# A cosine attention and gated MLP kernel on one core: the second half of each output tile is copied by ScalarE, and the planner may pick TensorE work out of order

## The chip, the cores and the metric

The kernel runs on one core of one Trainium2 chip. The metric is the device time in microseconds (us) of one launch. A profile of one execution gives what each engine did: TensorE (PE, its weight loads PEld), VectorE (DVE), ScalarE (ACT), GpSimd (POOL) and SyncE (SP), which issues most of the DMAs.

## The reference

The first part is attention with normalised queries and keys; the second is a two-matrix MLP with a gate of its own.

```python
q_n = q / (norm(q) + 1e-6);  k_n = k / (norm(k) + 1e-6)    # q, k, v: (8, 12, 448, 64)
attn = softmax(q_n @ k_n.T / tau)                          # tau = 0.1
x = (attn @ v).transpose(0, 2, 1, 3).reshape(3584, 768)
h = x @ w_in                                               # w_in: (768, 2048)
out = (h * cos(h)) @ w_out                                 # w_out: (2048, 768), out: (3584, 768) float32
```

## The kernel before, in words

**Work units.** There are 8 batches of 448 rows. The 12 heads of a batch are taken two at a time, which makes 48 pairs, six to a batch, numbered g = 0 to 47. For each pair, `scores` issues one short and three long groups of matmuls into the two PSUM buffers SC0 and SC1, and ScalarE exponentiates each group into the tile PX (L707). One pair later `attend` multiplies PX by the values into the PSUM buffer AV: two short groups R (L730) and three groups AV (L737), and the sums of the softmax beside them (L745, L753 and others). VectorE or ScalarE copies AV out to the tile xu; the reciprocals of the sums go through DRAM and come back spread over the partitions as the tile RB; GpSimd multiplies the two into the tile xT, the transposed input of the MLP (L877).

**The MLP.** When a batch's six xT pieces are done, and some pairs later, `m1` multiplies them by the first matrix (called M1 here; L887, full 128x128 matmuls), ScalarE takes the cosine (L916) and VectorE multiplies it in, giving the tile gT. The second matrix product (M2) works on 28 output tiles of 128 rows by 768 columns. M2 is the filler: `m2_fill` puts some steps of it between the score and attention groups of each pair. In the pairs the M2 steps are written for 64x64 quarters of TensorE (`m2_quarters`, L985): one step is four rows of 64x64 matmuls on both halves of the tile. The two halves (384 columns each) lie in the two banks of the one PSUM buffer MP, called PO and TP, and there is no second buffer for them. Near the end M2 uses full-size matmuls and more banks (L1014).

**The drain.** When the last step of tile t is done, `m2_drain` copies half 0 and half 1 from PSUM to the tile osb, and the DMA to the output (L956, issued by SyncE) waits for both halves. Both copies are VectorE instructions (L952), except the last piece of the last tile (t = 27), which ScalarE takes (L950). The first step of the next tile needs PO and TP, so it waits for both copies.

**The order.** Every instruction group is an `Op` with an engine, a cost in us, the tiles that it reads and writes, and for TensorE a mode: "Q" for 64x64 quarters, "C32" for 128x32 columns (AV and the sums), "F" for full size. `play` plans the whole program by these costs, engine by engine; `emit` writes the streams in the planned order with semaphore waits where tiles demand them. The order on ScalarE, VectorE, GpSimd and SyncE comes from due times (`o.late`), which are worked back from the planned TensorE starts in three passes. TensorE takes its operations in the order in which the program lists them: in the first stage (`free`, about the first 57 us: the first batch, its M1 and the loads) the planner may choose among the next 24, later it takes the head of the list alone. A choice is made by planned start: an operation further on is taken only if it starts more than `PATIENCE` = 0.1 us before the ones ahead of it. A change of mode costs `SWITCH` = 0.124, 0.094 or 0.107 us (into Q, C32, F) in the plan. `settled` adds a wait of `SETTLE` = 0.2 us after an earlier operation; it stands between the two R groups of a pair, and between the first and second half of a tile's M2 steps in quarters.

Of the kernel before, what the change touches and what calls it, by code (L numbers as in the profile page):

```python
# [6 lines left out]
ACT = mybir.ActivationFunctionType  # L7
# [5 lines left out]

PLAN = {
    "apart": 1,
    "ahead": (1, 2),
    "folded": (0, 1, 2, 3),
    "grid": {2: (16, 5, 6), 3: (11, 3, 4), 4: (8, 2, 3)},
# [44 lines left out]
class Program:  # L63
# [7 lines left out]
    DRAIN = {"ACT": 0.21, "DVE": 0.28, "POOL": 0.25, "SP": 0.3, "PE": 0.0}  # L71
    OVERLAP = {"ACT": 0.09, "DVE": 0.08, "POOL": 0.0, "SP": 0.0, "PE": 0.0}
    WINDOW = 24
    PATIENCE = 0.1
    TAKEOFF = {"SP": 1.85, "ACT": 1.85, "POOL": 1.6}
    LANDING = 0.45
# [79 lines left out]
    def play(self):  # L156
        ops = self.ops
        left = [len(o.deps) for o in ops]
        ready_at = [0.0] * len(ops)
        users = [[] for _ in ops]  # L160
        for o in ops:
            for y, k in o.deps:
                users[y.idx].append((o, k))
        free = {e: 0.0 for e in self.ENGINES}
        free["PE"] = free["SP"] = 0.7
        mode, port = None, 0.0
        flows = {"hw": [], "sw": []}
        clock = warm = 0.0
        self.gaps = []
        pe = [o for o in ops if o.eng == "PE"]  # L170
        waiting = {e: [] for e in self.ENGINES}
        for o in ops:
            if left[o.idx] == 0:
                waiting[o.eng].append(o)
        todo = len(ops)
        flying = held = 0
        room_at = 0.0

        def release(o, issued=False):
            for w, k in users[o.idx]:  # L180
                if o.dma is not None and (k is None) != issued:
                    continue
                left[w.idx] -= 1
                r = o.start if k is None else o.end + (self.SETTLE if k == "settled" else self.latency(o, w))
                if r > ready_at[w.idx]:
                    ready_at[w.idx] = r
                if left[w.idx] == 0:
                    waiting[w.eng].append(w)

        def flow(until):  # L190
            nonlocal clock, flying, held, room_at
            while clock < until:
                heads = [q[0] for q in flows.values() if q and q[0][0] <= clock + 1e-9]
                step = until - clock
                for q in flows.values():
                    if q and q[0][0] > clock + 1e-9:
                        step = min(step, q[0][0] - clock)
                total = sum(h[2] for h in heads) / (self.BOTH if len(heads) > 1 else 1.0)
                for h in heads:
                    step = min(step, h[1] * total / h[2])  # L200
                clock += step
                done = []
                for h in heads:
                    h[1] -= step * h[2] / total
                for q in flows.values():
                    if q and q[0][1] <= 1e-9:
                        done.append(q.pop(0))
                for h in done:
                    flying -= 1
                    if h[3].eng == "SP":  # L210
                        held -= h[3].descs // h[3].nd
                        room_at = clock + self.LANDING
                    if h[4]:
                        h[3].end = clock + self.LANDING
                        release(h[3])
                if done:
                    return True
            return False

        while todo:  # L220
            best = None
            for e in self.ENGINES:
                if e == "PE":
                    s = None
                    for o in pe[: self.WINDOW if pe and pe[0].free else 1]:
                        if o.free != pe[0].free:
                            break
                        if left[o.idx] == 0:
                            t = max(free[e], ready_at[o.idx])
                            if s is None or t < s - self.PATIENCE:  # L230
                                s, c = t, (t, 0, o)
                    if s is None:
                        continue
                else:
                    if not waiting[e]:
                        continue
                    f = free[e]
                    now = min(max(f, ready_at[o.idx]) for o in waiting[e])
                    o = min((o for o in waiting[e] if ready_at[o.idx] <= now + 1e-9), key=lambda o: (o.late, o.idx))
                    s = now  # L240
                    for w in waiting[e]:
                        if w.late < o.late - PLAN["margin"] and ready_at[w.idx] <= now + min(PLAN["hold"], 0.5 * o.cost):
                            o, s = w, max(f, ready_at[w.idx])
                    if e == "SP" and held and held + o.descs > self.ROOM:
                        continue
                    if e == "SP" and held + 2 * o.descs > self.ROOM:
                        s = max(s, room_at)
                    if o.lock:
                        s = max(s, port)
                    c = (s, 1, o)  # L250
                if best is None or c[:2] < best[:2]:
                    best = c
            if flying and flow(best[0] if best is not None else 1e9):
                continue
            s, _, o = best
            e = o.eng
            if e == "PE":
                pe.remove(o)
                if o.free:
                    self.gaps.append((max(free[e], 3.0), s))  # L260
                if mode is not None and mode != o.mode:
                    s += self.SWITCH[o.mode]
                mode = o.mode
            else:
                waiting[e].remove(o)
            o.start = s
            o.end = s + o.cost
            free[e] = max(free[e], o.end - self.OVERLAP[e])
            if o.lock:
                port = o.end  # L270
            todo -= 1
            if o.dma is None:
                release(o)
                continue
            release(o, True)
            clock = max(clock, s) if not flying else clock
            s += self.TAKEOFF[e] + o.lead
            if e == "POOL" and warm == 0.0:
                warm = s + self.COLD
            for n in range(o.nd):  # L280
                flows["sw" if e == "POOL" else "hw"].append(
                    [max(s + n * o.cost / o.nd, warm if e == "POOL" else 0.0), max(o.bulk / o.nd, 0.02), o.weight, o, n + 1 == o.nd])
                flying += 1
                if e == "SP":
                    held += o.descs // o.nd
        while flying:
            flow(1e9)
        self.span = max(o.end for o in ops)
# [102 lines left out]
def bass_cosine_attention__then__act_gcu_kernel(  # L391
# [10 lines left out]
    DM = NH * D  # L402
# [32 lines left out]
    def sbs(name, n, shape, dt):  # L435
        return [sb("%s%d" % (name, i), shape, dt) for i in range(n)]
# [22 lines left out]
    osb = sbs("osb", 3, [128, DM], F32)  # L459
# [486 lines left out]
    def m2_drain(t, hf, name, po, w):  # L946
        o, n, ends = t % 3, w[1] - w[0], t == B * S // 128 - 1
        dst, keys = osb[o].ap()[:, w[0] : w[1]], [("osb", o, y) for y in range(2)]
        if ends and w[1] == DM:
            act(lambda e: e.activation(dst, po[:, 0:n], ACT.Copy, bias=0.0), name + [("osb", o, 0)], [("osb", o, hf)], n, label="osb%d" % t)  # L950
        else:
            dve(lambda e: e.tensor_copy(dst, po[:, 0:n]), name, [("osb", o, hf)], n, label="osb%d" % t)  # L952
        if not ends and hf == 0:
            return
        c0, c1 = w if ends else (0, DM)
        fns = [lambda e, p0=p0, row=row: e.dma_start(  # L956
            bass.AP(out.tensor, row * DM + c0, [[NB * DM, BP], [1, c1 - c0]]), osb[o].ap()[p0 : p0 + BP, c0:c1]) for p0, row in segments(t)]
        for x, eng in enumerate(("SP", "ACT") if ends and hf else ("SP",)):
            dma(eng, fns[x : x + 1] if ends and hf else fns, [("osb", o, hf)] if ends else keys, [], "last" if x else "out%d" % o,
                n / DM if ends else 1.0, "out%d" % t, None, 1.0)  # L960
# [294 lines left out]
```

## Time and profile before

| | |
|---|---|
| median of 3 runs | 425.53 us (424.62 to 425.71) |
| span of the profiled execution | 424.5 us (the only time that the records give for it) |
| TensorE busy | 414.0 us, 98% |
| ScalarE busy | 274.1 us, 65% |
| VectorE busy | 189.0 us, 45% |
| GpSimd busy | 236.9 us, 56% |
| granted TensorE clock | 1.000 |
| copies to osb | VectorE 56, ScalarE 1 |

The span runs from the first to the last instruction. A group row of the profile gives an instruction's source line, engine, operation, output and input tiles with their shapes, the count, then the busy time, the mean duration in ns, and the idle time of the engine before it with what ended it. TensorE's busy share counts overlapping matmuls as busy, so small stalls between groups are seen better in the starts of successive groups than in the share.

### The profile page before, as it was taken

The numbers are of one execution on the slowest core, as the hardware profiler recorded it, in microseconds if no ns is written. First come the engines' busy times: TensorE is split into PE (matmuls) and PEld (weight loads), VectorE is DVE, ScalarE is ACT, GpSimd is POOL, SyncE is SP. The second block draws the span as 40 slices with busy tenths as digits, with TensorE's granted clock in tenths as the row PEclk, the third lists the DMA queues.
The fourth block names the chain that finished last, engine by engine and source line by source line (L and its number), as shares of the span: only waits on it lengthen the run. The fifth ranks groups of instructions, "written<-read, shape, count | busy, mean of one in ns | idle before, by whom it ended". The sixth has DMA issues, their size and how long they took to land.

```text
span 424.5 us, 13591 instructions
## 1 busy us (share of the span) xinstructions
PE 414.0 (98%) x6077; PEld 234.8 (55%) x6077; DVE 189.0 (45%) x250; ACT 274.1 (65%) x363; POOL 236.9 (56%) x189
## 2 busy tenths in 40 slices
PE   8899989999999999999999999999999999999997
PEld 3454556655556555655566455655566545555565
DVE  4564744555653086225733078122852144223521
ACT  5896578884897557876588556775488735713500
POOL 4999996897833794927493395806856042020000
PEclk9999999999999999999999999999999999999999
DMA  8999999999576999589655996569955930141023
GB/s 188 250 253 224 207 215 161 195 206 231 102 107 144 201 223 186 116 193 209 155 116 86 207 229 106 133 100 224 224 111 89 147 105 2 42 120 38 2 60 90
DMA packets 81034, 63.61 MB, mean 150 GB/s; under 512 B 45776, under 2 KB 75984, under 8 KB 80976
## 3 DMA queue, kind: packets, MB, share of 16 engines
q1 hardware_dynamic: 62768, 50.06, 56.8%
q0 software_dynamic: 18048, 12.59, 19.7%
q8 instruction: 48, 0.79, 0.8%
q10 hardware_dynamic: 160, 0.10, 0.1%
q14 instruction: 10, 0.08, 0.1%
HBM read 54.98 MB, written 11.13 MB: 156 GB/s over the span
## 4 chain that ended last, share of the span: by engine, by line
PE 73%; POOL 8%; DMA 6%; issue 4%; ACT 4%; SPq 3%; DVE 2%; ACTq 0%; POOLq 0%; DVEq 0%
PE MP L985 18%; PE SC L887 17%; PE AV L887 11%; PE SC L692 5%; PE AV L737 5%; POOL qks L643 4%; PE MP L1014 4%; POOL xT L877 3%; PE SC L1014 3%; DMA RB<-scr 3%; PE MP L887 2%; PE AV L730 2%; PE AV L763 1%; DMA qkT<-qks 1%; ACT PX L707 1%
## 5 line engine op out<-in xcount | busy, mean ns | idle before, releaser
L707 ACT ACTIVATE PX<-SC 128x448 bf16<-128x448 f32 (+1 forms) x192 | 153.2, 823 | 25.8 <-PE SC L692 15.6
L985 PE MATMUL MP<-W,gT 64*64 64x384 bf16 x2816 | 142.0, 323 | 0.8 <-DVE qkT L681 0.6
L985 PEld LDWEIGHTS MP<-W,gT 64*64 64x64 bf16 x2816 | 78.7, 107 | 34.5 <-issue 3.5
L643 POOL TENSOR_TENSOR qks<-raw,rn 128x896 bf16<-128x896 f32 (+1 forms) x48 | 79.6, 1680 | 31.8 <-ACT rn L635 31.6
L887 PE MATMUL SC<-xT,W 128*128 128x448 bf16 x444 | 90.2, 352 | 0.0
L877 POOL TENSOR_TENSOR xT<-xu,RB 128x448 bf16<-128x448 f32 x34 | 37.7, 1136 | 74.7 <-DMA RB<-scr 74.7
L604 POOL TENSOR_TENSOR sq<-raw 128x896 bf16<-128x896 f32 x44 | 73.8, 1694 | 8.3 <-DMA raw<-in_q_dram 7.7
L916 ACT ACTIVATE cosb<-SC,cst 128x896 f32<-128x896 f32 x37 | 37.2, 1006 | 49.0 <-PE SC L887 44.5
L887 PEld LDWEIGHTS SC<-xT,W 128*128 128x128 bf16 x444 | 43.4, 98 | 40.2
L887 PE MATMUL AV<-xT,W 128*128 128x448 bf16 x276 | 59.7, 353 | 1.7 <-POOL xT L877 1.7
L952 DVE COPY osb<-MP 128x384 f32<-128x384 f32 x50 | 25.9, 552 | 67.0 <-PE MP L985 56.4
L611 DVE TENSOR_REDUCE n<-sq 128x14 f32<-128x896 bf16 (+2 forms) x49 | 51.4, 1055 | 6.3 <-ACT sq L602 5.2
L692 PE MATMUL SC<-qkT 64*64 64x448 bf16 x576 | 52.1, 357 | 0.4 <-ACT PX L707 0.2
L918 DVE TENSOR_TENSOR gT<-SC,cosb 128x896 bf16<-128x896 f32 x37 | 40.3, 1088 | 23.2 <-ACT cosb L916 23.1
L916 ACT ACTIVATE cosb<-AV,cst 128x896 f32<-128x896 f32 x23 | 23.1, 1006 | 35.0 <-PE AV L887 32.0
L887 PEld LDWEIGHTS AV<-xT,W 128*128 128x128 bf16 x276 | 26.0, 98 | 29.1 <-POOL xT L877 5.1
L918 DVE TENSOR_TENSOR gT<-AV,cosb 128x896 bf16<-128x896 f32 x23 | 25.0, 1088 | 27.5 <-ACT cosb L916 27.4
L817 DVE COPY xu<-AV 128x896 f32<-128x896 f32 x20 | 21.7, 1083 | 30.4 <-PE AV L753 30.3
L737 PE MATMUL AV<-PX,va 128*32 128x448 bf16 x492 | 31.0, 356 | 0.0
L692 PEld LDWEIGHTS SC<-qkT 64*64 64x64 bf16 x576 | 16.5, 105 | 17.8 <-ACT PX L707 9.9
L730 PE MATMUL AV<-PX,va 64*64 64x224 bf16 x192 | 25.7, 262 | 0.2
L730 PE MATMUL AV<-PX,ones 64*64 64x224 bf16 x192 | 25.7, 262 | 0.0
(78 smaller groups left out, 361.7 us busy)
## 6 DMA issues: line engine op xcount, KB each, us to landing
raw<-in_k_dram SPq DMA_DIRECT2D x48, 224.0 KB, 6.4
raw<-in_q_dram SPq DMA_DIRECT2D x48, 224.0 KB, 7.1
out_dram<-osb SPq DMA_DIRECT2D x54, 192.0 KB, 3.4
va<-in_v_dram POOLq DMA_DIRECT2D x32, 192.0 KB, 8.9
RB<-scr SPq DMA_DIRECT2D x18, 336.0 KB, 4.8
W<-in_moe_w_in_dram POOLq DMA_DIRECT2D x4, 768.0 KB, 14.5
W<-in_moe_w_out_dram POOLq DMA_DIRECT2D x4, 768.0 KB, 19.1
RB<-scr SPq DMA_DIRECT2D x6, 224.0 KB, 4.3
```

What stands on the lines that cost most here:

```text
L604: pool(lambda e, x=x, y=y: e.tensor_tensor(y, x, x, ALU.mult), src_, dst, 0.1 + n * 1.78e-3, label="sq%d.%d" % (u, p)).pad = LATE if u > 1 ...
L611: dve(lambda e, w=w: e.tensor_reduce(out=n2v[i][:, 2 * p : 2 * p + 2, w], in_=sqv[p][:, :, w, :], axis=mybir.AxisListType.X, op=ALU.add), ...
L643: f = lambda e, s0=s0, s1=s1: e.tensor_tensor(qksv[i][:, p, s0:s1].rearrange("p s h d -> p h s d"), rawv[i][:, h, s0:s1, :], bass.AP(rn[i] ...
L692: m = e.matmul(SCv[z][BP * o : BP * o + BP, a, 0:S], t[r, c - 1 + (NT3 + 1) * o, 0:BP], t[r, :, BP : 2 * BP], start=True, stop=True)
L707: act(lambda e: e.activation(PHv[j] if c == 0 else PXv[j][:, c - 1], SCv[z][:, :, 0:n], ACT.Exp, scale=1.0 / TAU), ["SC%d" % z], [("PX", j ...
L730: m = e.matmul(to, w, PHv[j][r, a, :], start=(n == 0 and g not in PLAN["quarters"]), stop=False)
L737: t = e.matmul(AVv[o : o + 32, 0, 0:S], vav[y][:, 2 * p + a, c + 1, d : d + 32], PXv[j][:, c, a, :], start=False, stop=(c == NT3 - 1))
L877: pool(lambda e, p=p: e.tensor_tensor(xTv[b % 2][:, UP * i + p, :], xuv[:, u % 3, p, :], RBv[i][:, p, :], ALU.mult), [("RB", i, p), ("xa", ...
L887: t = e.matmul(ph[:, a, 0:S], W1v[:, order[c], 128 * n : 128 * n + 128], xTv[b % 2][:, order[c], :], start=(c == 0), stop=(c == NKC - 1))
L916: act(lambda e, ph=ph, cz=cz: e.activation(cosv[cz], ph[:, :, 0:S], ACT.Sin, bias=cst.ap()[:, 0:1], scale=1.0), names(gi) + ["cst0"], [("c ...
L918: dve(lambda e, ph=ph, cz=cz, gi=gi: e.tensor_tensor(gTv[:, 2 * gi : 2 * gi + 2, S * (b % 2) : S * (b % 2) + S], ph[:, :, 0:S], cosv[cz], ...
L985: r = e.matmul(POH[b][x : x + 64, 0:HW], gTv[k, y, col + x : col + x + 64], W2v[k, y, HW * b : HW * b + HW], start=(y == 0 and h == 0), st ...
```

## The change

Two edits. In `m2_drain`, half 1 of tiles 0 to 24 is copied by a ScalarE activation (Copy) instead of a VectorE copy; half 0 stays on VectorE. For these tiles the ScalarE copy is not ordered behind the VectorE copy. In `play`, after the first stage, TensorE's next operation may be picked among the next eight of the list by the same rule of planned starts, where a candidate's start now holds the cost of its change of mode.

```diff
 PLAN = {
     "apart": 1,
+    "halves": tuple(range(25)),
...
     WINDOW = 24
+    REACH = 8
     PATIENCE = 0.1
...
-                    for o in pe[: self.WINDOW if pe and pe[0].free else 1]:
+                    for o in pe[: self.WINDOW if pe and pe[0].free else self.REACH]:
                         if o.free != pe[0].free:
                             break
                         if left[o.idx] == 0:
                             t = max(free[e], ready_at[o.idx])
+                            if not o.free and mode is not None and o.mode != mode:
+                                t += self.SWITCH[o.mode]
                             if s is None or t < s - self.PATIENCE:
                                 s, c = t, (t, 0, o)
...
-                if mode is not None and mode != o.mode:
+                if o.free and mode is not None and mode != o.mode:
                     s += self.SWITCH[o.mode]
...
         dst, keys = osb[o].ap()[:, w[0] : w[1]], [("osb", o, y) for y in range(2)]
-        if ends and w[1] == DM:
-            act(lambda e: e.activation(dst, po[:, 0:n], ACT.Copy, bias=0.0), name + [("osb", o, 0)], [("osb", o, hf)], n, label="osb%d" % t)
+        if w[1] == DM and (ends or t in PLAN["halves"]):
+            act(lambda e: e.activation(dst, po[:, 0:n], ACT.Copy, bias=0.0), name + ([("osb", o, 0)] if ends else []), [("osb", o, hf)], n,
+                label="osb%d" % t)
         else:
             dve(lambda e: e.tensor_copy(dst, po[:, 0:n]), name, [("osb", o, hf)], n, label="osb%d" % t)
```

## The prediction, made before the changed kernel ran

> **What bounds the kernel now.** I first read the page's busy shares and its chain that ended last: TensorE is busy 98% of the 424.5 us span, and no other engine is over 65%. So only what TensorE waits for can be won. I then read who waits for whom on TensorE's weight loads (a load that waits holds up its matmul) from 57 us on, where both edits act. Columns: total us, times, longest.
>
> ```profile
> PEld SC L692 <- ACT PX L707: 8.1, 29, 0.5
> PEld AV L887 <- POOL xT L877: 5.1, 8, 1.0
> ...
> PEld MP L985 <- DVE osb L952: 2.5, 13, 0.2
> PEld MP L985 <- PE MP L985: 2.0, 6, 0.5
> ...
> PEld SC L700 <- DMA qkT<-qks: 1.0, 1, 1.0
> ```
>
> These are idle times of the load path, most of which lies under running matmuls. What TensorE itself loses is read from the starts of successive groups. First the drain, in the timeline of one tile (start, duration, engine, line):
>
> ```profile
> 226.81 0.27 PE L753 MATMUL AV<-PX,ones 128*32 128x224 bf16 x4
> 227.01 0.38 PE L692 MATMUL SC<-qkT 64*64 64x448 bf16 x4
> 227.31 1.01 PE L985 MATMUL MP<-W,gT 64*64 64x384 bf16 x20
> ```
>
> ```profile
> 226.23 1.02 DVE L952 COPY osb<-MP 128x384 f32<-128x384 f32 x2 [2.56 <-PE MP L985]
> ```
>
> ```profile
> 225.06 1.59 ACT L707 ACTIVATE PX<-SC 128x448 bf16<-128x448 f32 x2 [0.25 <-PE SC L700]
> 227.13 0.92 ACT L814 ACTIVATE xu<-AV 128x896 f32<-128x896 f32 x1 [0.47 <-PE AV L753]
> ```
>
> The two VectorE copies end at 227.25, and the next tile's M2 starts at 227.31, 0.30 after the score group ahead of it. Where a drain isn't waited for, the same step takes 0.21:
>
> ```profile
> 116.19 0.38 PE L692 MATMUL SC<-qkT 64*64 64x448 bf16 x4
> 116.40 0.66 PE L985 MATMUL MP<-W,gT 64*64 64x384 bf16 x12
> ```
>
> So a late drain costs TensorE 0.09 us, not the 0.2 of the load row: AV, sums and a score group already cover the rest. ScalarE is free from 226.65 to 227.13 in that place.
>
> Next the waits inside M2. Two runs of 24 M2 matmuls, the first with the change from a tile's first to its second half inside, the second without:
>
> ```profile
> 62.92 1.41 PE L985 MATMUL MP<-W,gT 64*64 64x384 bf16 x24
> ...
> 81.88 1.14 PE L985 MATMUL MP<-W,gT 64*64 64x384 bf16 x24
> ```
>
> **Edit one, the copies.** 25 copies leave VectorE: 25 x 0.557 us (the median of L952) = 13.9 of its 189 us. That engine bounds nothing, so this by itself is worth nothing. ScalarE gets 25 copies of 128x384. No such row exists; the 128x192 copy of L950 took 331 ns and the 128x896 copy to xu (L814) 917 ns, so by the line between them 0.331 + 192 x 0.586/704 = 0.49 us each, 12.3 us in all. What counts is when both halves are out. In the example ScalarE finishes its exponential at 226.65, would copy until 227.14 (0.09 earlier, 227.05, if the copy starts under the tail of the one before, as its successive rows do), and VectorE's one copy ends at 226.79. So PO and TP come free 0.1 to 0.2 us sooner than 227.25, and the 0.09 goes. I went through the 13 late drains in this way. In 12 ScalarE has an idle place of 0.46 to 1.2 us just where the copy wants to go; in the thirteenth (262.49) two short instructions fill 262.40 to 263.00, then 0.70 is idle, enough for a copy that ends at or ahead of 263.51. So 13 x 0.09 = 1.2 us come off.
>
> Not all of it reaches the end. The M1 at 241 waits for xT from a chain that begins at the xu copy at 222.58 and goes through SyncE, DRAM and GpSimd; the M1 at 341 likewise. Two late drains lie inside each of these chains, so 4 x 0.09 = 0.36 only makes the xT wait longer. At 292 it is otherwise, for the chain there goes through the copies themselves and the SyncE queue behind them, as the chain of waits shows:
>
> ```profile
> 280.89 1.03 DVE osb L952 x2
> ...
> 281.94 0.50 SPq L956
> ...
> 283.13 1.77 SPq L873
> 284.95 5.21 DMA RB<-scr
> 290.22 3.32 POOL xT L877 x3
> ```
>
> The output DMA waits for both halves and the DMA for RB is queued behind it, so an earlier half moves xT too. Net of edit one's gain: 0.8 us (0.8 to 1.2).
>
> Its cost: a ScalarE copy stands in a queue with the exponentials behind it, and TensorE's scores need those to have emptied SC0 or SC1. In the 13 places idle time takes it. At the drains at 115.11 and 126.14 there is none: exponentials run back to back until 116.16 and 127.30, so either one of them is 0.4 to 0.49 later or M2 is up to 0.25 later. Bounds 0 to 0.49 each, since the scores that follow have slack of their own (0.46 idle at 116.2); I take 0.1 each, near the row with slack: +0.2. The copies at 144.61 and 289.62 meet a table load (until 145.27 and 290.28), but the next M2 is 17 us off. Those after 372 lie where ScalarE is nearly idle. The output DMAs keep their place on SyncE and are released no later.
>
> The Trainium skill (Perfetto Trace Analysis, "Optimizing Scalar/DVE Operations") recommends moving work to ScalarE when VectorE is saturated. VectorE is at 45% and ScalarE at 65%, so by that rule this move loads the busier engine; what it would cost is the second rival below.
>
> **Edit two, the choice among eight.** It can win only where the head is planned more than 0.1 us late and one of the next seven is free. Place by place:
> - *The half change of an M2 tile* (six waits, 2.0 us of load idle). The planner knows this wait, 0.2. Inside a run of M2 steps the next score group can go first. From the rows above 1.41 - 1.14 = 0.27; at 109.65 twelve matmuls took 0.92 against 0.66, 0.26. Two others (259.1, 358.4) lose 0.15, just over the patience, two more 0.05. I count 0.26 + 0.26 + half of 0.3 = 0.65 (0 to 0.8).
> - *The wait for qkT* at 83.67: 0.8 us between group starts over the usual. M2 steps stand behind it, so it can be filled if the plan sees the DMA late; the trace can't tell. 0 to 0.8, I take 0.2, as SyncE's queue there holds six output DMAs and the plan's waits are built from fixed costs.
> - *Scores waiting for an exponential* after 57 us: 0.38 at 60.33, 0.14 and 0.09 later. 0 to 0.6, I take 0.2.
> - *xT* (5.1 us of load idle, the largest): nothing. The operations behind a waiting M1 step are more M1 steps for the same pieces; M2 is over twelve steps away.
>
> Its cost: an operation taken early may be of another mode. In the rows above, the score group at 227.01 starts 0.20 after a 224-column group, which takes 0.09 where no change of mode follows (a 224-column group at 225.52 is followed in the same mode at 225.61, 0.09 later), so a change costs 0.11 us, and an operation put between two of another mode costs two. The rule charges the way in and not the way back. Bounds: none, or two in each of 36 pairs, 7.2 us. AV never waits for PX after 57 us by the waits view, so there is little reason to break its groups: I take one such insertion, +0.2.
>
> **Sum.** -0.8 + 0.2 - 0.65 - 0.2 - 0.2 + 0.2 = -1.45 us on the span of 424.5. The records give no other time of the profiled execution; the median is 1.03 above its span, which I leave as it is: 425.53 - 1.45 = 424.1.
>
> A measurement of this kernel can tell some 0.3%, 1.3 us, from no change, so the sum stands just over that edge.
>
> **Rivals.**
> 1. *The waits come back elsewhere.* Faster TensorE only waits longer for xT, and the plan finds nothing to reorder: edit one's 0.8 less the 0.2 to 0.4 at dense places gives 425.0. For: each xT wait follows a chain of 15 to 18 us that no edit shortens, and the saved pieces are small. Against: M2's half-change waits are in the plan as well as in the trace.
> 2. *ScalarE's queue.* A copy that waits for M2's last step holds the exponentials behind it, and scores stall for SC0 or SC1. In 105 to 144 us ScalarE is busy 33.3 of 39 us; with four copies 35.2. If each of the 21 copies inside the attention stretches put its 0.4 (0.49 less 0.09 overlap) ahead of an exponential that TensorE waits for in half of the cases, that is +4.2 - 0.8, 428.9; if in a quarter, +2.1 - 0.8, 426.8. It is slower from a fifth on. Against: 13 places with idle time.
> 3. *Changes of mode and M2 spent early.* The choice among eight takes M2 steps ahead of AV groups, at 0.2 us for two changes; in 20 of 36 pairs +4.0 less 1.45 gives 428.1. It decides from about seven pairs on. The Trainium skill (TensorEngine Tiling (Array Packing), "Key Properties") says that changing the tiling mode drains TensorE; by that rule every such step costs, and the trace agrees, with the 0.11 us above.
> 4. *More than I count.* The plan fills the qkT wait and the score waits whole: 1.2 + 0.8 + 0.8 + 0.6 = 3.4 less 0.2, 422.3.
>
> **Chances.** The forecast 0.42, rival 1 0.23, rival 2 0.13, rival 3 0.12, rival 4 0.10. The forecast's own range is 423.2 to 425.0, so about 0.08 of it lies within 0.3%, and part of rivals 2 and 3 does too (0.03). Faster 0.42 - 0.08 + 0.10 = 0.44; same 0.23 + 0.08 + 0.03 = 0.34; slower 0.22. The range takes in rival 4's end and rivals 2 and 3 up to 427.8, leaving out some 0.2.
>
> **What would show it.** The osb copies split: some 31 on VectorE, 26 on ScalarE at 0.49. The row of M2 waiting for osb falls from 2.5 to under 1. The row of M2 waiting for its own first half falls from 2.0 to under 1. The xT row stays or grows by some 0.4. Wrong: scores waiting for PX over 8.1 or a new wait for ScalarE's osb (rival 2); more changes between L985 and L737 (rival 3); a change in the xT row of over 1 us, for then the reordered plan moved the chains and not the drains, which I have not priced.

## The result, and the profile after

The changed kernel takes 422.5 us (421.58 to 424.6, 7 runs) against 425.53: ratio 0.9937, 95% interval 0.9913 to 0.9962. Compared once more on another occasion it was 422.56 against 424.61, ratio 0.9952 (0.9934 to 0.9970). So it gains 2 to 3 us, where 1.45 were forecast. 422.5 lies inside the stated range, but under the forecast's own 423.2 to 425.0 and next to the 422.3 of rival 4 (more than counted, chance 0.10); the second comparison's gain of 2.05 lies inside the forecast's own range. "Faster" had the largest chance, 0.44, with rival 4 in it. A ratio here compares all runs of two kernels; it is not the quotient of the two medians and differs from it by up to 0.2%.

The first profile of it was taken on the longest of its seven executions (424.6 us, span 422.8); a second one has a span of 420.2, and it is the one shown here. New line numbers are four or five higher: M2 is L990, VectorE's osb copy L957, ScalarE's L954, the score groups L696 and L704, xT L881.

The waits of the weight loads from 57 us on, the same view as before the change (total us, times, longest):

```profile
PEld SC L696 <- issue: 6.4, 23, 0.3
PEld AV L891 <- POOL xT L881: 2.8, 5, 0.7
...
PEld SC L696 <- ACT PX L711: 2.4, 9, 0.3
...
PEld MP L990 <- PE MP L990: 1.0, 3, 0.5
...
PEld SC L696 <- ACT osb L954: 0.3, 1, 0.3
```

The row of M2 waiting for osb (2.5 us, 13 times) is gone, and so is the row of scores waiting for qkT (1.0). M2's wait for its own first half is halved, 2.0 to 1.0. The row for xT is 2.8 where it was 5.1. Scores waiting for PX fell from 8.1 to 2.4, but most of that went over to the first row, waits for nothing that the profile names. Before the change this row was

```profile
PEld SC L692 <- issue: 1.9, 7, 0.3
```

so the two together are 8.8 after 10.0. The ScalarE copies are named as the cause of a wait only in the last row: 0.3 us of load idle, once.

The place shown before the change, tile 11, in TensorE's, VectorE's and ScalarE's timelines:

```profile
225.43 0.38 PE L696 MATMUL SC<-qkT 64*64 64x448 bf16 x4
225.64 0.98 PE L990 MATMUL MP<-W,gT 64*64 64x384 bf16 x20
```

```profile
224.65 0.56 DVE L957 COPY osb<-MP 128x384 f32<-128x384 f32 x1 [2.56 <-PE MP L990]
```

```profile
223.49 1.59 ACT L711 ACTIVATE PX<-SC 128x448 bf16<-128x448 f32 x2 [0.25 <-PE SC L704]
224.98 0.48 ACT L954 ACTIVATE osb<-MP 128x384 f32<-128x384 f32 x1
225.55 0.92 ACT L818 ACTIVATE xu<-AV 128x896 f32<-128x896 f32 x1
```

M2 now starts 0.21 after the score group, not 0.30, with the last half out at 225.46 (224.98 + 0.48). ScalarE's copy begins under the tail of the exponential and ends before the copy to xu may begin: it sits in the 0.47 us that was idle.

The first profile shows one wait of a size that no other profile here has. At 181.8 M2's weight loads waited 0.95 us for the drain, and the half that was late is VectorE's:

```profile
180.78 0.18 DVE L871 TENSOR_REDUCE rcp<-sums 128x14 f32<-128x28 f32 x1 [3.56 <-DMA sums<-xu]
180.99 0.24 DVE L874 RECIPROCAL rcp<-rcp 128x14 f32<-128x14 f32 x1
181.15 0.49 DVE L957 COPY osb<-MP 128x384 f32<-128x384 f32 x1
```

The copy ends at 181.64; ScalarE's half was out at 180.73. (The profile puts the wait down to the xu copy on ScalarE, which ended at 181.74, but M2 uses nothing that this copy reads or writes.) The planned order puts the sum and reciprocal ahead of the copy, and in that execution their DMA landed late. The kernel before has the same order there: in its second profile M2 starts 0.42 after the score group at this place, and 0.30 or 0.31 at the twelve other late drains. The prediction had looked at what is queued behind the copy on ScalarE and not at what is queued ahead of the one left on VectorE.

### The profile page after: what moved, and what is told of

Same layout as the page of the kernel before. It is cut to its first block, busy times and chain, and to the rows that moved or that the text cites. A ratio compares the mean times of both kernels' runs of the same rounds, so it can differ in the third digit from the quotient of the medians.

```text
span 422.8 us, 13649 instructions
## 1 busy us (share of the span) xinstructions
PE 412.1 (97%) x6077; PEld 237.6 (56%) x6077; DVE 177.3 (42%) x225; ACT 283.0 (67%) x388; POOL 237.0 (56%) x189
## 4 chain that ended last, share of the span: by engine, by line
PE 84%; POOL 6%; issue 4%; ACT 2%; DMA 1%; DVE 1%; SPq 1%; POOLq 0%; ACTq 0%
PE MP L990 23%; PE SC L891 19%; PE AV L891 12%; PE SC L696 6%; PE AV L741 6%; PE MP L1019 4%; POOL qks L647 3%; PE SC L1019 3%; PE MP L891 2%; PE AV L734 2%; PE AV L767 2%; POOL xT L881 2%; DMA raw<-in_q_dram 1%; PE AV L749 1%; PE AV L1019 1%
## 5 line engine op out<-in xcount | busy, mean ns | idle before, releaser
L990 PE MATMUL MP<-W,gT 64*64 64x384 bf16 x2816 | 141.9, 323 | 1.4 <-ACT xu L818 0.7
L990 PEld LDWEIGHTS MP<-W,gT 64*64 64x64 bf16 x2816 | 81.3, 107 | 31.7 <-issue 3.5
L881 POOL TENSOR_TENSOR xT<-xu,RB 128x448 bf16<-128x448 f32 x34 | 37.8, 1137 | 66.8 <-DMA RB<-scr 66.7
L696 PE MATMUL SC<-qkT 64*64 64x448 bf16 x576 | 52.8, 357 | 0.2
L957 DVE COPY osb<-MP 128x384 f32<-128x384 f32 x26 | 14.4, 555 | 67.6 <-PE MP L990 56.1
L696 PEld LDWEIGHTS SC<-qkT 64*64 64x64 bf16 x576 | 16.9, 105 | 17.1 <-ACT PX L711 6.2
```

Source lines behind the costliest of these rows:

```text
L696: m = e.matmul(SCv[z][BP * o : BP * o + BP, a, 0:S], t[r, c - 1 + (NT3 + 1) * o, 0:BP], t[r, :, BP : 2 * BP], start=True, stop=True)
L881: pool(lambda e, p=p: e.tensor_tensor(xTv[b % 2][:, UP * i + p, :], xuv[:, u % 3, p, :], RBv[i][:, p, :], ALU.mult), [("RB", i, p), ("xa", ...
L990: r = e.matmul(POH[b][x : x + 64, 0:HW], gTv[k, y, col + x : col + x + 64], W2v[k, y, HW * b : HW * b + HW], start=(y == 0 and h == 0), st ...
```

## The experiments

Each was timed against the kernel before, with one profile. There were three such comparisons, in which the kernel before took 424.61, 425.01 and 425.25 us; where an expectation gives a time, it stands on 425.5, so the ratio is what to compare. "Strict order" means that the choice among eight is set back to the head of the list.

**Each edit alone.** The copies split for 25 tiles, strict order:

```diff
-    REACH = 8
+    REACH = 1
```

> The copies split, TensorE's order as before (the choice is back to the head of the list). Theory A (the two edits add up): the 13 late drains go, 1.2 to 1.5 us, and the xT wait at 293 shrinks because the planner now issues the RB DMA ahead of an output DMA: 424.0 to 424.4 against 425.5, ratio 0.9965 to 0.998. The qkT wait at 84 us (0.8) and M2's half-change waits (0.88 over six) stay. Theory B (the choice among eight carries it): within 0.5 us of before, since what the drains give is lost to xT waits. Theory C (the copies carry it): 422.5 to 423.2, the whole gain.

Measured: 423.98 against 424.61, ratio 0.9988 (0.9970 to 1.0007), less than the 0.9965 to 0.998 of theory A, though the interval reaches into it. The choice among eight alone:

```diff
-    "halves": tuple(range(25)),
+    "halves": (),
```

> The choice among eight, all copies but the last on VectorE as before. Theory A: three of the M2 half-change waits and the qkT wait at 84 us go (0.24 + 0.15 + 0.15 + 0.8), the 13 late drains stay: 424.0 to 424.4, ratio 0.9965 to 0.998. Theory B: 422.5 to 423.2. Theory C: within 0.5 us of before.

Measured: 423.98, ratio 0.9982 (0.9962 to 1.0002). The changed kernel in the same comparison:

> The changed kernel once more, for a second profile. The first profile shows one wait of 0.9 us at 181.8, where VectorE's osb copy stood behind a reciprocal that waited for a DMA, and the profiled execution was the longest of seven. If that wait belongs to the plan it is here again at nearly the same place; if it is that execution's, it is gone and the span is about 420.5. Time 422.5 either way.

Measured: 422.56, ratio 0.9952, span 420.2; the wait at 181.8 is gone, so its size was that execution's.

Each edit alone gives 0.5 to 0.8 us with an interval of about 0.8 to either side, both together 2.0. By its time alone neither is clear of no change. Theories B and C, that one edit carries the whole, are unlikely, but the intervals of each edit alone still touch that of both (0.9934 to 0.9970). That the two add up fits, and the times can't show more. The profiles are sharper than the times, as they show which waits each edit takes. The waits of the weight loads with the copies alone:

```profile
PEld MP L990 <- PE MP L990: 2.0, 6, 0.5
PEld SC L704 <- DMA qkT<-qks: 1.4, 1, 1.4
```

and with the choice alone:

```profile
PEld MP L990 <- DVE osb L957: 2.4, 13, 0.2
...
PEld MP L990 <- PE MP L990: 1.0, 3, 0.5
```

The first has no osb row and keeps the other two in full; the second keeps the 13 late drains, halves the half-change row and has no qkT row. Neither touches what the other takes.

**Which copies count.** The split for the 13 late tiles alone, strict order:

```diff
-    "halves": tuple(range(25)),
+    "halves": (5, 7, 8, 10, 11, 12, 13, 14, 15, 17, 18, 19, 20),
```

> The copies split for the 13 tiles alone whose drain TensorE waited for (5, 7, 8, 10 to 15, 17 to 20), order on TensorE as before. If the gain of the copies is those 13 waits, this gives the same as the copies split for all 25 (424.0 to 424.4). If it is relief of VectorE or the earlier output DMAs of all tiles, it gives half of it or less.

Measured: 423.93, ratio 0.9982 (0.9965 to 1.0000), no osb row for M2 in the profile. In the middle that is no less than with 25, which speaks for those waits and against relief of VectorE; but the interval would also hold half the gain, so it is the profiles, here and in the next experiment, that decide. With the choice among eight added:

> Both edits, but the copies split for the 13 late tiles alone. If the copies of the other tiles only load ScalarE, this is as fast as the changed kernel or up to 0.5 us faster (421.8 to 422.6 against 422.5); if they help (output DMAs released earlier), up to 0.5 us slower.

Measured: 423.89 against 425.25, ratio 0.9968 (0.9949 to 0.9986); 25 tiles had 0.9952 (0.9934 to 0.9970). In the middle that is 0.7 us slower than with 25, but the intervals overlap: the 12 other copies neither cost nor give anything that this shows, and this version is not better than the changed kernel.

**Side by side or just ScalarE.** For the same 13 tiles both halves on ScalarE, strict order:

```diff
-        if w[1] == DM and (ends or t in PLAN["halves"]):
+        if ends and w[1] == DM or t in PLAN["halves"]:
```

> For the 13 tiles whose drain was late, both halves are copied by ScalarE, one after the other, TensorE's order as before. If the gain of the copies comes from the two halves leaving side by side, it is lost here and more: two ScalarE copies of 0.49 that start 0.2 to 0.4 us later than VectorE's did, so each of the 13 late drains costs 0.2 to 0.5 us where it cost 0.11 before: 1 to 5 us slower than before, ratio 1.003 to 1.012. If it is VectorE's relief or ScalarE's speed that pays, this is as fast as the split for 13 tiles (0.998).

Measured: 425.66 against 425.01, ratio 1.0011 (0.9985 to 1.0036), under the 1.003 to 1.012 expected, though the interval reaches into it. The waits:

```profile
PEld MP L990 <- ACT osb L954: 3.9, 11, 0.4
...
PEld AV L891 <- POOL xT L881: 1.3, 3, 0.5
```

The osb wait is back, named for ScalarE, and larger than the 2.5 before. By the starts of successive groups M2 starts 0.46 to 0.48 after the score group at 11 tiles, where 0.21 is usual and the late drains before had 0.30: TensorE loses 0.25 us at each of 11 tiles instead of 0.09 at 13, 2.8 against 1.2. So it is the two engines at work side by side that frees the buffer in time. In the middle the time rose by 0.5 us and not by the 1.6 of these drains; the xT row is small in this profile (1.3), and more of that row stands below.

**What the choice among eight does, by place.** Only up to the M1 of the second batch, and only from there on, the copies as before:

```diff
+        limit = min(o.idx for o in pe if o.label.startswith("M1 1."))
...
-                    for o in pe[: ... else self.REACH]:
+                    for o in pe[: ... else self.REACH if pe and pe[0].idx < limit else 1]:
```

> The choice among eight up to the M1 of the second batch (about 57 to 87 us) and the list's order from there on; all copies but the last on VectorE. Theory A: the qkT wait at 84 us (0.8) and the half-change wait at 63.7 (0.24) go, which is most of what the choice brings: 0.8 to 1.2 us less than before, ratio 0.997 to 0.9985. Rival: the early part costs as much as it gives (more steps between score groups, 0.6 us of unnamed waits at 67 seen in two profiles), ratio 1.000.

Measured: 423.85 against 425.01, ratio 0.9968 (0.9943 to 0.9993). In the profile the second batch's M1 starts at 85.6, 29.0 us after the first M2; before the change it was 86.7, 30.0 after. The qkT row is gone. Of the five profiles with the choice in this part, three have the M1 at 29.0 or 29.1. In the other two, the first of the changed kernel and that of the choice alone, it is 29.9: a stop that the profile doesn't name, 0.87 us of load idle at 67, takes most of the gain back. The second profile of the changed kernel has 0.15 there, so the size of this stop goes with the execution.

> The choice among eight only from the M1 of the second batch on, all copies but the last on VectorE. Theory A: the half-change waits at 259 and 358 (0.15 each) go, nothing else: 0.3 us less than before, ratio 0.999 to 1.000. Rival: it moves xT chains, and the xT row changes by 1 us or more either way.

Measured (`>=` in place of `<`): 424.17, ratio 0.9971 (0.9944 to 0.9999), which doesn't fit the 0.3 us expected well, though the interval takes it in and reaches almost to no change. In the profile the waits at 259 and 358 (0.15 each) are gone, the wait for qkT is 1.3 in the load row, and the xT row is 2.7, inside what executions without the choice show. What the late part gives beyond the 0.3 stays open. Each part alone came out with a larger gain than the whole choice (0.9982), which shows how little these times resolve.

**How the qkT wait went.** The prediction thought of M2 steps put in front of the waiting score. SyncE's queue tells otherwise. The transposing DMA that the score at 83.67 waited for, in the kernel before:

```profile
76.76 1.24 SPq L873 DMA_DIRECT2D RB<-scr  x2
78.11 1.80 SPq L660 DMA_TRANSPOSE qkT<-qks  x1
```

and in the changed kernel, where the last transposing DMA of this stretch is

```profile
73.33 2.23 SPq L664 DMA_TRANSPOSE qkT<-qks  x1
...
80.77 1.24 SPq L877 DMA_DIRECT2D RB<-scr  x2
```

The same DMA, the fourth transposing one from 59 us on, is issued 4.8 us sooner, ahead of loads and of the RB DMA that it stood behind. Before it landed 5.5 us after its issue, at 83.6; now it lands after 5.3, at 78.6, four us ahead of its score. TensorE's own order is the same in both kernels from 78 us to the M1, so nothing was put in front of the score. Before:

```profile
81.88 1.14 PE L985 MATMUL MP<-W,gT 64*64 64x384 bf16 x24
83.67 0.29 PE L700 MATMUL SC<-qkT 64*64 64x224 bf16 x4 [0.64 <-DMA qkT<-qks]
```

and after:

```profile
81.78 1.15 PE L990 MATMUL MP<-W,gT 64*64 64x384 bf16 x24
82.75 0.27 PE L704 MATMUL SC<-qkT 64*64 64x224 bf16 x4
```

All five profiles with the choice in the early part and a patience of 0.1 have the early DMA and no wait; the six profiles with the list's order there and SyncE's order untouched have the DMA behind RB and the wait. By the planner's code the link is the due times: a few TensorE operations taken in another order at 60 to 70 us change them, and SyncE's order with them; this link was not tried by itself. To see whether SyncE's order alone is enough, the kernel before with two transposing DMAs moved one place or two ahead:

```diff
-                [("qkT", j, 0), ("qkT", j, 1)], "T%d" % j, 1.4, "T%d" % g, None, 10.0)
+                [("qkT", j, 0), ("qkT", j, 1)], "T%d" % j, 1.4, "T%d" % g, None, 10.0).bias = -3.0 if g < 13 else 0.0
```

> Neither edit: TensorE, VectorE, ScalarE and GpSimd have the order of the kernel before, and on SyncE two transposing DMAs (the ones issued at 71.8 and 78.1 us before) get due times 3 us earlier, which puts each one place or two ahead. Theory (the qkT wait of 0.8 us at 84 us is the order on SyncE, and the choice among eight removed it by moving the due times, not by filling it with M2 steps): the wait at 84 us goes here too, and M1 of the second batch starts 0.5 to 1 us earlier than 86.7; time 0.3 to 0.8 us less than before. Rival (it takes other work on TensorE to cover it): the wait stays at 0.8 or more, time as before.

Measured: 425.34 against 425.25, ratio 0.9988 (0.9966 to 1.0010). The DMA was issued 1.2 us sooner, at 76.92, but landed 6.7 us after its issue instead of 5.5, so at 83.6 again, and its score starts when it did before, at 83.68:

```profile
83.11 0.52 PE L990 MATMUL MP<-W,gT 64*64 64x384 bf16 x8 [0.20 <-issue]
83.68 0.29 PE L704 MATMUL SC<-qkT 64*64 64x224 bf16 x4
```

The qkT row fell from 1.0 to 0.4 only because TensorE stopped ahead of it, until 83.11, in a wait that the profile doesn't name. The M1 came no sooner, at 87.13, 30.3 us after the first M2. So this edit did not bring the data earlier and decides nothing between theory and rival. That the wait went because the data came 5 us sooner is shown by the changed kernel's own timeline; that SyncE's order alone would do it in the kernel before is not shown.

**The third rival, made to happen.** A smaller patience in the changed kernel:

```diff
-    PATIENCE = 0.1
+    PATIENCE = 0.05
```

> The changed kernel with a patience of 0.05 us in place of 0.1, which is below the plan's cost of a change of mode (0.094 to 0.124): now every head that needs a change is put behind a ready step of the running mode, so AV groups wait for M2 and score steps. This is rival 3 of the prediction made to happen. Theory (the order of the list is good where TensorE doesn't wait, and the patience above the cost of a change keeps it): 3 to 10 us slower than the changed kernel, 425.5 to 432. Rival (grouping by mode saves changes): as fast as the changed kernel or faster.

Measured: 434.9 against 425.01, ratio 1.0214 (1.0175 to 1.0252). That is 9.9 over the kernel before and so some 12 us over the changed kernel, more than the 3 to 10 expected. The waits:

```profile
PEld AV L891 <- POOL xT L881: 3.2, 3, 2.5
PEld AV L734 <- DVE xu L821: 2.8, 5, 0.8
...
PEld AV L767 <- DVE xu L821: 1.6, 2, 1.2
```

Grown are the waits for xu, which are 0.2 and 0.3 us in the two profiles of the kernel before: the AV groups come late, so their copy out of the one AV buffer comes late, and the next pair's first AV groups wait for it. The number of changes of mode did not rise (79 from 57 us on, counted by group starts, against 83), so the price is not the changes themselves; that it is the postponed work is read from these waits.

**How far a profile repeats.** The kernel before once more:

> The changed kernel's code with both edits set to nothing, the program of the kernel before, for a second profile of it. The waits that the plan makes should be where they were: 13 late drains at 0.11, half-change waits at 63.7, 110, 259 and 358, and about 0.8 at 84 us for qkT. If the xT row is 2.9 us again, the fall to 1.4 with both edits is theirs; if it is near 1 us, the xT row goes with the execution and not with the kernel. Ratio 1.000.

Measured: 425.2 against 425.25, ratio 1.0004 (0.9985 to 1.0022), span 422.5 where the first profile had 424.5. The waits:

```profile
PEld MP L990 <- DVE osb L957: 2.6, 13, 0.3
...
PEld MP L990 <- PE MP L990: 2.0, 6, 0.5
PEld AV L891 <- POOL xT L881: 1.7, 4, 0.6
...
PEld SC L704 <- DMA qkT<-qks: 1.1, 1, 1.1
```

The sums of these rows repeat to 0.1 us, except the xT row, which hangs on DMAs: it is 1.7 where it was 5.1. So the fall of that row from 5.1 to 2.8 can't be put down to the change. Over the six profiles with the 13 late drains it was 5.1, 1.7, 2.7, 0.9, 1.0 and 2.7 (mean 2.4), with the split copies 3.6, 3.2, 3.1, 2.8 and 3.7 (mean 3.3), and with the longer drains of both halves on ScalarE 1.3. This is the direction that the prediction gave: what the drains free is partly waited away at xT. The spread within one kernel is too large to call it shown.

## Why the prediction was right, point by point

- *13 late drains at 0.09.* Right in kind, count and size: the row is gone, tile 11 shows 0.30 to 0.21, the split alone leaves the rest untouched, and both halves on ScalarE bring it back. One of the 13, at 234.8 in the second profile, still has 0.30, with no cause named. The copies are 31 on VectorE and 26 on ScalarE, as said. The net of 0.8 after what xT takes back fits 0.5 and 0.8 us measured for the two split kernels, whose intervals reach from no gain to 1.3 and 1.5.
- *The copy at 0.49 us.* Measured 0.485 (L954). Next to it VectorE's copy is 0.558.
- *ScalarE's queue, +0.2.* Over-priced: nothing of it is seen. In 111 to 140 us, which holds both back-to-back places, ScalarE is busy 24.8 instead of 24.0 us, and the rows of scores (L696) waiting for PX or for nothing named are together 8.8, after 10.0 before; with the copies alone they are 9.7. The second rival did not come. The Trainium skill (Perfetto Trace Analysis, "Optimizing Scalar/DVE Operations") gives a saturated VectorE as the case for moving work to ScalarE. Here VectorE is at 45% and the late drains still go, since what counts is not either engine's load but when the later half is out.
- *M2's half change, -0.65.* By group starts the loss went from 0.88 to 0.34, -0.54: the waits at 63.7, 259 and 358 are gone. The one at 110 stayed, so 0.26 counted for it did not come, while the two near the patience went whole.
- *The qkT wait, -0.2.* This is the term that was mis-sized. It took 0.8 in the first and 0.9 in the second profile before, and is absent in every profile with the choice in the early part and a patience of 0.1. The step that failed is the reading that only M2 steps placed ahead of the score could cover it: TensorE's order there stayed as it was, and the DMA landed 5 us sooner, in an order on SyncE that the planner had re-made.
- *Scores waiting for an exponential, -0.2.* 0.61 to 0.44 by group starts.
- *Changes of mode, +0.2.* None: 83 before and after. The patience is above the planned price of a change into C32, so AV groups are not put off. The rule of the Trainium skill (TensorEngine Tiling (Array Packing), "Key Properties"), that a change of mode drains TensorE, had no further changes to act on.
- *The sum.* With the measured sizes it is 0.8 + 0.5 + 0.85 + 0.2 = 2.35 off and nothing on, against 2.0 and 3.0 us in the two comparisons. The 0.8 is the forecast's own net, which the times allow but don't fix. So the drains and the half changes went in the way that was forecast and the qkT wait in another, and the missing 0.9 is 0.65 of the qkT wait and 0.4 of costs that did not arise, less 0.15 of the half changes.
- *The base.* The span of 424.5 was read as 1.0 below the median. The profile of the changed kernel has its own time beside it, 424.6 for a span of 422.8: 1.8 lie around the span. By that, the execution profiled before was a long one, and its xT row the longest of all profiles here. The forecast took differences, so this hurt little, but it made xT look like the largest thing to win. For the same reason the 4.3 us between the two spans shown (424.5 and 420.2) are not the gain: 1.5 of them are the wait for xT by group starts.
- *The signs.* The prediction named a change of over 1 us in the xT row as a sign of being wrong. It came, 5.1 to 2.8. As the kernel before changes this row by 3.4 between two of its own profiles, the sign can't tell.

## What to carry to other kernels

When a buffer without a twin must be emptied, split the copy over two engines and look for the idle place where the second engine can take its part; the load of that engine over the whole span did not decide it here. When a planner is allowed to reorder one engine, price the queues whose due times follow from that order too: here the largest single wait went because a DMA was issued 4.8 us sooner, and a patience set below the price of a change of mode cost 12 us. Take two profiles before a wait that hangs on DMAs goes into a sum.

## What the hardware showed that was not expected

In four profiles TensorE stopped for 1.27, 0.97, 0.72 and 0.48 us near 114 us in the middle of four matmuls that have no wait between them, as here with the choice alone:

```profile
114.10 0.26 PE L734 MATMUL AV<-PX,va 64*64 64x224 bf16 x1
115.46 0.25 PE L734 MATMUL AV<-PX,ones 64*64 64x224 bf16 x1 [1.10 <-issue]
```

The profile names no releaser; transfers of the instruction queues lie in the 3 us ahead of it each time, but such transfers pass without a stop elsewhere. What it is was not tried and stays open. It is of the size of the effects measured here, so single profiles differ by it.
